# Attention inside a fused kernel: the six parts of `a` are added before one product with ones, and the maxima of phi move to another buffer

## The chip, the core and the metric

The kernel runs on one core of one Trainium2 chip. The core has a matrix engine (TensorE, written PE in the profile, with its weight loads as PEld), three engines for elementwise work (VectorE = DVE, ScalarE = ACT, GpSimd = POOL), and a sync engine (SP) whose queue issues all DMAs here. Each engine runs its own instruction list in order and waits on the others through semaphores. The metric is device time in microseconds.

## What is computed

Three stages follow each other. Only the first is touched; the other two are two feed-forward layers on its output (4608 tokens, width 512, hidden width 2048).

```
q, k, v: [8, 8, 576, 64]      phi: [8, 8, 576, 32]         (batch, heads, seq, ...)
a    = exp(phi - max over seq of phi);  a = a / (sum over seq of a + 1e-9)
k_m  = a^T k   [32, 64];  v_m = a^T v   [32, 64]           per batch and head
attn = softmax((q k_m^T) / 8);   x = attn v_m
y    = layer2(layer1(x))         layer1: (h - tanh h) w_out,  layer2: elu(h) w_out
```

The kernel leaves `a` undivided, and multiplies `k_m` and `v_m` by the reciprocal of the sum of `a` over the sequence afterwards.

## The kernel before, in words

**Units.** The attention is cut into 16 units; unit u is one batch and four of its heads. The 576 positions of the sequence lie as 96 partitions by 6 parts (`c`), so phi and `a` are tiles of 96 x 6 x 4 x 32. Unit 0 has tiles of its own (`at0`); units 1 to 15 share one set (`at1`).

**A unit's steps.** `unit` is a Python generator that emits instructions and yields; each `yield` ends a step. In order, for u >= 2 (`spaced`):

1. `top`, `cmax` (L120 to L122, DVE): maximum of phi over the six parts.
2. nothing (L126).
3. `mT` (PE transpose), `nmax`, `dmax` (DVE).
4. `bmax` (PE, L135); a yield of its own follows.
5. `bm` (ACT), then `a = phi - bm` (POOL for u >= 2, DVE for units 0 and 1).
6. load of the next phi.
7. `a = exp(a)` (ACT, L147).
8. `km`: 24 matmuls a^T [k v] into the PSUM tile `km` (L156), then six matmuls of `a[:, c]` with a tile of ones into its last columns (L159), which gives the sum of `a`. The trace shows every fp32 matmul as two records, so L156 is 48 records a unit, L159 12.
9. `rs`, `kk`, `vbd` (DVE, L165 to L171), the scaled k_m and v_m read from `km`.
10. and on: load of the next k and v; `pq`, `qT` twice; `kT_ps` (transposes of `kk` and `vbd`, L189 and L190), `kT`, `vm`; `sc` (scores) and its transpose; again `pq` twice and `sc`; `smax`; `exp`; a multiplication `s` (L215, POOL); `pT` (L218, DVE); `phl` (L222 on ACT, L223 on POOL); nothing; the stores of p.

Units 0 and 1 have no empty steps: their steps 8 and 9 are one.

**Rounds.** A driver calls one step of every live unit per round, in the order in which the units started. Unit u starts at a fixed round:

```
(0, 1, 7, 13, 19, 25, 32, 39, 45, 52, 58, 65, 78, 85, 92, 99)[u]
```

So step s of unit u runs in round start + s - 1, and three or four units are live at a time, a round's steps of the older unit ahead of those of the younger. The first 19 rounds are the prologue (with the conversion of the first weights, L48 to L60). After it, layer 1 runs as 64 blocks of two halves; each half emits an `h_unit` (PE, L343), its nonlinearity (ACT L354 to L357, POOL `v` L362, DVE L367 to L369, later ACT L375 and POOL `g` L376), two `x_unit` (PE L388, copied out by ACT L395), sometimes two `vw_half` (PE L328, ACT L331, DVE L333), and two rounds of units.

**Order.** The order of each engine's list is that of emission; nothing reorders it. A tile is taken from a pool by a tag; a tag of the pool `at_wk` has one buffer, so a new tile of the tag waits until every instruction that reads the old one is done, also one that is emitted after the new tile's first write. `top` has the tag `pT`, shared with the tile `pT`; `kk` and `vbd` have tags of their own. The PSUM tiles `mT`, `bmax`, `km`, `pq`, `kT_ps`, `sc`, `x_ps` and `vw_ps` share one pool of three buffers (after the prologue).

Of the kernel before, what the change touches and what calls it, by code (L numbers as in the profile page):

```python
# [8 lines left out]
F32 = mybir.dt.float32  # L9
# [4 lines left out]
ALU = mybir.AluOpType  # L14
# [4 lines left out]
B, H, S, D, M = 8, 8, 576, 64, 32  # L19
# [43 lines left out]
class Attention:  # L63
# [43 lines left out]
    def unit(self, u, nxt, eng, first_p=None):  # L107

        nc, wk, sm = self.nc, self.wk, self.sm
# [3 lines left out]
        kv, a, kT = self.kv, self.a, self.kT  # L113
        ps_tile = lambda shape, name: self.ps.tile(shape, F32, tag="m", name=name)

        ph = self.loaded.pop((u, "phi"))
        row = lambda name: wk.tile([128, 4, M], F32, tag="cmax", name=name)
        cmax = row("cmax")[:96]
        top = wk.tile([128, S], F32, tag="pT", name="top")[:96, :12 * M].rearrange("p (h c m) -> p h c m", h=4, c=3)
        nc.vector.tensor_tensor(top, ph[:, :, 0:3], ph[:, :, 3:6], op=ALU.max)  # L120
        nc.vector.tensor_tensor(cmax, top[:, :, 0], top[:, :, 1], op=ALU.max)
        nc.vector.tensor_tensor(cmax, cmax, top[:, :, 2], op=ALU.max)  # L122
        yield
        spaced = u >= 2
        if spaced:
# [10 lines left out]
        if spaced:  # L136
# [5 lines left out]
                          op=ALU.subtract)  # L142
# [9 lines left out]
        km = ps_tile([128, 2 * D + 2], "km")  # L152
        kmv = km[:, :2 * D].rearrange("p (t d) -> p t d", t=2)
        for c in range(6):
            for h in range(4):
                nc.tensor.matmul(kmv[32 * h:32 * h + 32], lhsT=a[:, c, h, :], rhs=kv[:, :, h, c, :],  # L156
                                 start=(c == 0), stop=(c == 5))
        for c in range(6):
            nc.tensor.matmul(km[:, 2 * D:], lhsT=a[:, c].rearrange("p h m -> p (h m)"), rhs=self.ones[:, :2],  # L159
                             start=(c == 0), stop=(c == 5))  # L160
        if spaced:
            yield
        rs = sm.tile([128, 1], F32, tag="rs", name="rs")
        twice = lambda t: kmv[:, t].rearrange("p (o d) -> p o d", o=1).to_broadcast([128, 2, D])
        nc.vector.tensor_scalar(rs, km[:, 2 * D:2 * D + 1], GUARD, None, op0=ALU.add)  # L165
        nc.vector.reciprocal(rs, rs)
        kk = wk.tile([128, 2, D], F32, tag="kk", name="kk")
        nc.vector.tensor_scalar(kk, twice(0), rs, None, op0=ALU.mult)
        vbd = wk.tile([128, 2, D], F32, tag="vbd", name="vbd")
        for j in range(2):  # L170
            nc.vector.tensor_scalar(vbd[:, j], kmv[:, 1], rs, self.pmask[:, j:j + 1], op0=ALU.mult, op1=ALU.mult)  # L171
        yield
# [2 lines left out]
        for pr in range(2):  # L175
# [25 lines left out]
            for hq in range(2):  # L201
                nc.tensor.matmul(sc[64 * hq:64 * hq + 64], lhsT=kT[:, 2 * pr + hq].rearrange("p c m -> p (c m)"),
                                 rhs=qT[:, hq].rearrange("p c q -> p (c q)"), start=True, stop=True)
# [13 lines left out]
        pT = wk.tile([128, S], F32, tag="pT", name="pT")  # L217
# [285 lines left out]
def moe_kernel(tc, q, k, v, phi, w1, w2, w3, w4, out):  # L503
    nc = tc.nc
    with ExitStack() as top, tc.manual_schedule():
# [96 lines left out]
        for u in range(2 * B):  # L602
            units.at((0, 1, 7, 13, 19, 25, 32, 39, 45, 52, 58, 65, 78, 85, 92, 99)[u], unit(u))
# [252 lines left out]
```

## Time and profile before

| | |
|---|---|
| time, median of 3 runs | 1750.95 us (1750.49 to 1754.13) |
| the profiled execution | 1751.26 us, span of its instructions 1749.5 us |
| PE / PEld busy | 1637.8 us (94%) / 1513.9 us (87%) |
| DVE busy | 1222.6 us (70%) |
| ACT busy | 954.2 us (55%) |
| POOL busy | 760.9 us (43%) |
| mean granted TensorE clock | 0.970 |

Attention takes part in the first 480 us or so of the span; the last unit's maxima are taken at 403.6 us and its `pT` is read at 478.4 us. A duration in a row is that of one instruction or of a merged run of like ones; "x12" is their number. A wait in brackets is the idle time of the engine ahead of the instruction, with the instruction that ended it.

### The profile page before, as it was taken

How to read it: one execution, taken by the hardware profiler on the slowest of the kernel's cores; microseconds unless marked ns; L12 is line 12 of the kernel's file. 1: busy time of each engine (PE TensorE's matmuls, PEld its weight loads, DVE VectorE, ACT ScalarE, POOL GpSimd, SP SyncE). 2: the span in 40 equal slices, each digit the busy share in tenths (PEclk: the TensorE clock that was granted, in tenths of full speed). 3: DMA queues.
4: the chain of work that ended last, by engine and by line, in shares of the span. 5: the costliest groups of instructions: out<-in, count | busy, mean ns of one | idle time of the engine just before them, and what ended most of it. 6: DMA issues, size and time to landing. Idle time of an engine off the chain costs nothing.

```text
span 1749.5 us, 30362 instructions
## 1 busy us (share of the span) xinstructions
PE 1637.8 (94%) x11632; PEld 1513.9 (87%) x11632; DVE 1222.6 (70%) x1821; ACT 954.2 (55%) x1713; POOL 760.9 (43%) x537
## 2 busy tenths in 40 slices
PE   5668989988998999999989999999999999999998
PEld 3557878887898999999989999999999999999997
DVE  5769666778899999998965555555555555555554
ACT  2456666677878888888863333333333333333332
POOL 2245545546666667676752222222222222222222
PEclk7669999999999999999999999999999999999999
DMA  8765555467566456666578312211212212111110
GB/s 213 198 177 148 179 158 181 147 199 232 187 211 200 167 182 208 215 223 208 203 230 316 130 60 61 61 54 56 61 61 61 61 61 61 58 52 58 58 31 25
DMA packets 140936, 238.42 MB, mean 136 GB/s; under 512 B 8184, under 2 KB 102392, under 8 KB 138744
## 3 DMA queue, kind: packets, MB, share of 16 engines
q1 hardware_dynamic: 140792, 236.49, 43.3%
q8 instruction: 92, 1.51, 0.4%
q14 instruction: 52, 0.43, 0.1%
HBM read 159.78 MB, written 75.50 MB: 134 GB/s over the span
## 4 chain that ended last, share of the span: by engine, by line
PE 75%; DVE 10%; ACT 5%; DMA 5%; issue 3%; POOL 2%; ACTq 0%; DVEq 0%; POOLq 0%; SPq 0%
PE h_ps L444 23%; PE o_ps L481 23%; PE x_ps L388 15%; PE h_ps L343 8%; PE vw_ps L328 3%; DVE s L368 2%; DMA w_dram<-wst 2%; DVE vw L333 1%; DMA raw<-in_moe_w_in_dram 1%; DMA phi<-in_phi_dram 1%; DVE h_ps L367 1%; DVE s L369 1%; PE km L156 1%; ACT t L354 1%; ACT big L357 1%
## 5 line engine op out<-in xcount | busy, mean ns | idle before, releaser
L388 PE MATMUL x_ps<-g,w 128*128 128x288 f32 x3072 | 442.8, 298 | 13.7 <-ACT x L395 6.7
L470 POOL TENSOR_TENSOR e<-hm,e 128x512 fp32r<-128x512 f32 x144 | 186.5, 1295 | 587.0 <-ACT e L469 442.6
L444 PEld LDWEIGHTS h_ps<-x,wi 128*128 128x128 f32 x3456 | 429.8, 190 | 11.7
L388 PEld LDWEIGHTS x_ps<-g,w 128*128 128x128 f32 x3072 | 421.5, 190 | 18.6 <-ACT x L395 8.0
L444 PE MATMUL h_ps<-x,wi 128*128 128x256 f32 x3456 | 433.2, 282 | 0.0
L481 PE MATMUL o_ps<-wo,e 128*128 128x512 f32 x1728 | 423.8, 394 | 0.7 <-POOL e L470 0.7
L481 PEld LDWEIGHTS o_ps<-wo,e 128*128 128x128 f32 x1728 | 314.9, 188 | 64.9 <-POOL e L470 1.1
L455 ACT ACTIVATE t_ps<-hm 128x512 f32<-128x512 f32 x144 | 86.7, 602 | 514.3 <-DVE hm L454 514.3
L362 POOL TENSOR_TENSOR v<-t,u 128x576 f32<-128x576 f32 x128 | 183.9, 1437 | 197.6 <-ACT u L355 163.9
L343 PE MATMUL h_ps<-p,vw 128*128 128x288 f32 x1536 | 235.8, 304 | 7.9 <-DVE s L369 6.3
L376 POOL TENSOR_TENSOR g<-s,g 128x576 fp32r<-128x576 f32 x128 | 199.0, 1555 | 96.1 <-ACT g L375 91.1
L461 DVE SCALAR_TENSOR_TENSOR hm<-hm,t_ps 128x512 f32<-128x512 f32 x144 | 99.1, 688 | 200.6 <-ACT hm L456 200.6
L343 PEld LDWEIGHTS h_ps<-p,vw 128*128 128x128 f32 x1536 | 217.0, 194 | 12.9 <-issue 7.9
L454 DVE TENSOR_SCALAR hm<-h_ps 128x512 f32<-128x512 f32 x144 | 99.6, 692 | 138.5 <-PE h_ps L444 138.5
L368 DVE SCALAR_TENSOR_TENSOR s<-s,v 128x576 f32<-128x576 f32 x128 | 139.9, 1093 | 3.7 <-POOL v L362 2.6
L354 ACT ACTIVATE t<-h_ps 128x576 f32<-128x576 f32 x128 | 83.2, 650 | 72.7 <-PE h_ps L343 28.4
L369 DVE COPY_PREDICATED s<-big,h_ps 128x576 f32<-128x576 uint32 x128 | 106.6, 833 | 12.0 <-ACT u L355 0.5
L333 DVE TENSOR_TENSOR vw<-vw_ps,vw 64x512 fp32r<-64x512 f32 x128 | 87.8, 686 | 36.5 <-ACT vw L331 34.5
L356 ACT ACTIVATE s<-u,bias 128x576 f32<-128x576 f32 x128 | 99.5, 778 | 24.0 <-POOL g L376 14.6
L328 PE MATMUL vw_ps<-w,vm 128*128 128x256 f32 x480 | 78.9, 304 | 28.2 <-ACT x L395 14.7
L463 DVE TENSOR_TENSOR hm<-hm,h_ps 128x512 f32<-128x512 f32 x144 | 99.0, 687 | 5.0
L462 DVE SCALAR_TENSOR_TENSOR hm<-hm,t_ps 128x512 f32<-128x512 f32 x144 | 98.9, 687 | 4.9
(85 smaller groups left out, 1827.5 us busy)
## 6 DMA issues: line engine op xcount, KB each, us to landing
x_dram<-x SPq DMA_DIRECT2D x128, 288.0 KB
xr<-x_dram SPq DMA_DIRECT2D x72, 512.0 KB
p<-p_dram SPq DMA_DIRECT2D x62, 576.0 KB
raw<-in_moe_w_in_dram SPq DMA_DIRECT2D x32, 512.0 KB
raw<-in_moe_w_out_dram SPq DMA_DIRECT2D x32, 512.0 KB
w_dram<-wst SPq DMA_DIRECT2D x32, 512.0 KB
kv<-in_k_dram SPq DMA_DIRECT2D x16, 576.0 KB
kv<-in_v_dram SPq DMA_DIRECT2D x16, 576.0 KB
```

The costliest lines, as they stand in the source:

```text
L328: nc.tensor.matmul(ps[:, kc], lhsT=vm[:, a, p, :], rhs=wi[:, b, p, :], start=(i == 0), stop=(i == 2))
L333: nc.vector.tensor_tensor(lo, src, r32(hi), op=ALU.subtract)
L343: nc.tensor.matmul(ps[:, j, :NB], lhsT=vw[a][:, kc, 128 * j:128 * j + 128], rhs=p[:, kc, b, :], start=(k == 0), stop=(k == 5))
L354: nc.scalar.activation(t, w[0], ACTF.Tanh)
L362: nc.gpsimd.tensor_tensor(v, t, u, op=ALU.mult)
L368: nc.vector.scalar_tensor_tensor(s, s, G_B, v, op0=ALU.add, op1=ALU.mult)
L369: nc.vector.copy_predicated(s, big.bitcast(U32), d)
L376: nc.gpsimd.tensor_tensor(g[:, 1], s, r32(g[:, 0]), op=ALU.subtract)
L388: nc.tensor.matmul(ps, lhsT=wo[pg][:, a, j, 128 * dm:128 * dm + 128], rhs=g[:, b, j, :], start=(k == 0), stop=(k == 11))
L444: nc.tensor.matmul(ps[:, j], lhsT=w3[:, a, kc, 128 * j:128 * j + 128], rhs=x[:, b, kc, :], start=(k == 0), stop=(k == 11))
L470: nc.gpsimd.tensor_tensor(e[:, 1], hm, r32(e[:, 0]), op=ALU.subtract)
L481: nc.tensor.matmul(self.acc[n][tg], lhsT=e[:, a, j, 128 * tg:128 * tg + 128], rhs=w4[:, b, j, :], start=(pg == 0 and j == 0 and i == 0), s ...
```

## The change

The maximum over the six parts of phi is taken in three DVE instructions of another shape, into a tile `top` of half the size that has the tag `kk`. After the 24 matmuls of `km`, three additions (on GpSimd for u >= 2, on DVE for units 0 and 1) sum the six parts of `a` into a tile `asum`, also of the tag `kk`; for u >= 2 a new `yield` follows; then one matmul of `asum` with ones takes the place of the six. `kk` and `vbd` become the two halves of one tile of the tag `kk`.

```
-        top = wk.tile([128, S], F32, tag="pT", name="top")[:96, :12 * M].rearrange("p (h c m) -> p h c m", h=4, c=3)
-        nc.vector.tensor_tensor(top, ph[:, :, 0:3], ph[:, :, 3:6], op=ALU.max)
+        pair = lambda name: wk.tile([128, 2, 4, M], F32, tag="kk", name=name)
+        top = pair("top")[:96].rearrange("p c h m -> p h c m")
+        nc.vector.tensor_tensor(top, ph[:, :, 0:2], ph[:, :, 2:4], op=ALU.max)
+        nc.vector.tensor_tensor(top, top, ph[:, :, 4:6], op=ALU.max)
         nc.vector.tensor_tensor(cmax, top[:, :, 0], top[:, :, 1], op=ALU.max)
-        nc.vector.tensor_tensor(cmax, cmax, top[:, :, 2], op=ALU.max)
         yield
...
-        for c in range(6):
-            nc.tensor.matmul(km[:, 2 * D:], lhsT=a[:, c].rearrange("p h m -> p (h m)"), rhs=self.ones[:, :2],
-                             start=(c == 0), stop=(c == 5))
+        asum = pair("asum")[:96]
+        add = nc.gpsimd if spaced else nc.vector
+        add.tensor_tensor(asum, a[:96, 0:2], a[:96, 2:4], op=ALU.add)
+        add.tensor_tensor(asum, asum, a[:96, 4:6], op=ALU.add)
+        add.tensor_tensor(asum[:, 0], asum[:, 0], asum[:, 1], op=ALU.add)
+        if spaced:
+            yield
+        nc.tensor.matmul(km[:, 2 * D:], lhsT=asum[:, 0].rearrange("p h m -> p (h m)"), rhs=self.ones[:96, :2],
+                         start=True, stop=True)
         if spaced:
             yield
...
-        kk = wk.tile([128, 2, D], F32, tag="kk", name="kk")
+        kkv = pair("kk").rearrange("p c h m -> p c (h m)").rearrange("p t (o d) -> p t o d", o=2)
+        kk, vbd = kkv[:, 0], kkv[:, 1]
         nc.vector.tensor_scalar(kk, twice(0), rs, None, op0=ALU.mult)
-        vbd = wk.tile([128, 2, D], F32, tag="vbd", name="vbd")
```

## Rows read from the trace of the kernel before

**Rows 1.** Busy time by stretch: the stretch in us from the span's start, its length, busy us (and instructions) of PE, PEld, DVE, ACT and POOL, the granted clock of TensorE as a share of full speed, the DMA share and GB/s.

```profile
0.00:61.50 61.50, 31.53 (x244) 22.64 (x244) 40.89 (x92) 18.84 (x42) 16.71 (x19) 0.65 0.80 202
...
400.00:480.00 80.00, 72.73 (x612) 67.21 (x611) 69.70 (x109) 63.32 (x122) 49.27 (x35) 1.00 0.65 212
...
61.50:480.00 418.50, 360.68 (x3006) 325.88 (x3006) 318.14 (x517) 283.35 (x555) 217.44 (x152) 0.95 0.60 181
480.00:1749.50 1269.50, 1245.56 (x8382) 1165.42 (x8382) 863.59 (x1214) 652.05 (x1117) 526.77 (x368) 0.99 0.36 118
```

**Rows 2.** The chain of work that ended last: its shares by line over the stretch 61.5 to 480 us, and three of its pieces of L159 (start, us, what). The last two are the first and the last of seven pieces of 1.43 us between 150 and 480 us.

```profile
by line: PE x_ps L388 14.5%; PE h_ps L343 10.2%; issue 7.6%; PE vw_ps L328 6.7%; DVE s L368 4.9%; PE km L156 3.1%; PE km L159 3.0%; DVE h_ps L367 2.9%; ACT big L357 2.9%; DVE vw L333 2.8%; ACT t L354 2.7%; DVE s L369 2.6%; DMA q<-in_q_dram 
...
122.94 2.65 PE km L159 x12
...
158.72 1.43 PE km L159 x12
...
435.60 1.43 PE km L159 x12
```

**Rows 3.** The matmuls with ones as one group of the costliest groups: records, busy us, mean ns of one, idle time before.

```profile
L159 PE MATMUL km<-ones,a 128*128 128x2 f32 x192 | 28.2, 275 | 0.0
```

**Rows 4.** Who waited for whom between 61.5 and 480 us, one line of DVE's and one of POOL's: us in total, times, the longest us.

```profile
DVE top L120 <- POOL phl L223: 20.1, 7, 7.0
...
POOL v L362 <- ACT u L355: 92.5, 29, 6.3
```

**Rows 5.** Instructions in order of time around the first step of unit 6 (its `top`): start, us, engine, line.

```profile
122.88 2.72 PE L159 MATMUL km<-ones,a 128*128 128x2 f32 x12
123.09 0.77 DVE L218 STREAM_TRANSPOSE pT<-s 128x576 f32<-128x576 f32 x1
...
126.88 0.68 PE L181 MATMUL pq<-ident,q 96*128 96x96 f32 x3
...
129.42 1.40 POOL L223 TENSOR_TENSOR phl<-pT,phl 128x576 fp32r<-128x576 f32 x1 [5.50 <-ACT phl L222]
...
130.86 0.56 DVE L120 TENSOR_TENSOR top<-phi 96x384 f32<-96x384 f32 x1 [7.00 <-POOL phl L223]
```

**Rows 6.** Instructions in order of time: `top` of units 10 and 12, and `top` of unit 14 with the `km` of unit 13 behind it.

```profile
246.47 0.55 DVE L120 TENSOR_TENSOR top<-phi 96x384 f32<-96x384 f32 x1 [4.68 <-POOL phl L223]
...
323.61 1.76 DVE L120 TENSOR_TENSOR top<-phi 96x384 f32<-96x384 f32 x1 [2.87 <-POOL phl L223]
...
373.87 0.54 DVE L120 TENSOR_TENSOR top<-phi 96x384 f32<-96x384 f32 x1
...
375.14 1.52 PE L156 MATMUL km<-kv,a 128*32 128x128 f32 x48
...
376.58 1.50 PE L159 MATMUL km<-ones,a 128*128 128x2 f32 x12
...
377.94 1.83 PE L388 MATMUL x_ps<-g,w 128*128 128x288 f32 x12
```

**Rows 7.** Durations in ns (shortest, median, longest) of single lines, for sizes: the subtraction of phi on POOL and on DVE, a POOL subtraction of the weights, and the maxima on DVE.

```profile
L141 POOL TENSOR_TENSOR a<-phi,bm x14: 1809/1856/2180, 37.5 to 425.0; 96x768 f32<-96x768 f32 x14
L141 DVE TENSOR_TENSOR a<-phi,bm x2: 954/954/955, 9.9 to 12.4; 96x768 f32<-96x768 f32 x2
...
L60 POOL TENSOR_TENSOR wst<-cv_a,wst x6: 1278/1289/1302, 399.5 to 475.7; 128x512 fp32r<-128x512 f32 x6
...
L120 DVE TENSOR_TENSOR top<-phi x16: 542/555/2029, 4.3 to 403.6; 96x384 f32<-96x384 f32 x16
...
L122 DVE TENSOR_TENSOR cmax<-cmax,top x16: 286/287/1530, 5.2 to 404.9; 96x128 f32<-96x128 f32 x16
```

**Rows 8.** The stretch 130 to 480 us: busy time of the engines as in rows 1, and the DVE instruction of L368 as a group (count, busy us, mean ns) and by its shortest, median and longest ns.

```profile
130.00:480.00 350.00, 314.12 (x2664) 287.74 (x2663) 269.63 (x431) 248.39 (x487) 188.25 (x131) 0.99 0.59 179
...
L368 DVE SCALAR_TENSOR_TENSOR s<-s,v 128x576 f32<-128x576 f32 x44 | 53.8, 1223 | 2.8 <-POOL v L362 1.7 <-ACT big L357 1.1
...
L368 DVE SCALAR_TENSOR_TENSOR s<-s,v x44: 739/759/3359, 133.2 to 477.6; 128x576 f32<-128x576 f32 x44
```

**Rows 9.** Waits of PE for a free PSUM buffer, 61.5 to 480 us: us in total, times, the longest us.

```profile
PE vw_ps L328 <- ACT x L395: 7.4, 10, 1.5
PE x_ps L388 <- ACT x L395: 6.7, 6, 1.4
...
PE vw_ps L328 <- DVE rs L165: 2.2, 2, 1.6
```

**Rows 10.** How long one unit (unit 9) holds its PSUM tile `km`: from the first matmul into it to the last read of it.

```profile
243.06 1.52 PE L156 MATMUL km<-kv,a 128*32 128x128 f32 x48
...
251.04 0.58 DVE L171 TENSOR_SCALAR vbd<-km,rs,pmask 128x64 f32<-128x64 f32 x2
```

**Rows 11.** The prologue: a piece of the chain (the DMA of phi for unit 2), three ACT instructions around the end of the prologue in order of time, and the wait of PE there.

```profile
16.53 11.69 DMA phi<-in_phi_dram
...
60.10 0.62 ACT L58 ACTIVATE w<-cv_a 128x512 fp32r<-128x512 f32 x1
...
61.18 0.28 ACT L196 ACTIVATE vm<-kT_ps 128x128 fp32r<-128x128 f32 x1
...
63.39 0.59 ACT L331 ACTIVATE vw<-vw_ps 64x512 fp32r<-64x512 f32 x1 [1.93 <-PE vw_ps L328]
...
PE vw_ps L328 <- ACT vm L196: 5.3, 1, 5.3
```

## The prediction

> **What bounds the kernel now.** I read the busy time by stretch first. Up to 61.5 us PE is busy for half of the time; from 61.5 to 480 us, where 14 of the 16 units run between the blocks of layer 1, it is busy 360.7 of 418.5 us (86%); from 480 us on 1245.6 of 1269.5 us (98%), with work that the change doesn't touch [rows 1]. So whatever the attention stretch gains or loses goes to the end unshrunk, and inside the stretch there are 58 us in which PE waits. The chain of waits comes next: between 61.5 and 480 us it changes from PE to DVE and ACT and back within every block, and the matmuls with ones hold 3.0% of it, 12.6 us [rows 2]. No single engine sets the end there: in the last 80 us PE is busy 91% and DVE 87% [rows 1]. What DVE waits for I read from its waits: 20.1 us in front of `top`, all on POOL's `phl` [rows 4].
>
> **Matmuls with ones.** 192 records become 32 (12 to 2 a unit), 28.2 us of PE busy time [rows 3] becomes about 28.2 x 2/12 = 4.7. What counts is what lies on the chain: one unit at 2.65 us and seven at 1.43 us [rows 2]; 10/12 of 2.65 + 7 x 1.43 = 12.7 is 10.5 us. The others end behind DVE or DMA work: unit 0's and unit 1's lie under the DMA of phi that the next `top` waits for, 16.53 to 28.22 us [rows 11]. The paths beside PE are close behind (DVE at 87%), so I take 9 of the 10.5; bounds 3 and 10.5.
>
> **Maxima.** Before, 384 and twice 128 elements a partition: 0.555 + 2 x 0.287 = 1.13 us [rows 7]. After, twice 256 and once 128; by the line through 0.287 (128) and 0.555 (384) 256 cost 0.42, so again 1.13. Nothing on DVE.
>
> **The wait of `top`.** This is where the change is least obvious. Seven `top`s wait for `phl` because they write the buffer of `pT`. That `top` waits even for readers emitted after it is to be seen at unit 6: `pT` of unit 3 is written in the same round just ahead, `phl` is emitted a round later, and DVE stands still from 123.86 to 130.86 us [rows 5]. In the changed kernel `top` is out of that buffer, so the 20.1 us go [rows 4]. But it is now in the buffer of `asum`, and the same thing happens there. Unit u emits `asum` in round start + 7; the matmul that reads it is behind the new yield, in round start + 8. Where unit u + 1 starts 7 rounds after unit u (u = 5, 6, 8, 10, 12, 13, 14), its `top` is emitted in round start + 7 too, after `asum`, so `top` takes the buffer next and DVE must wait for a matmul that PE comes to a round later. Where the gap is 6 or 13, `top` is ahead of `asum` or far behind it, and waits for nothing new. Seven waits go, seven come.
>
> Their size: at unit 14 DVE reaches `top` at 373.87 us, ahead of unit 13's `km` on PE, which ends at 376.58 [rows 6]. PE then has an `x_unit` (1.8 us) and a `pq` (0.68 us at the lower clock of [rows 5], some 0.4 here) before the matmul of `asum`: about 378.8, so 4.9 us of DVE standing still where there was no wait. Worked out in the same way from the time at which DVE reaches `top` and from PE's list up to the next round, the seven are 1.7 (unit 6, instead of 7.0), 2, 3.5, 3.6, 2.5, 4.9 and 3.1: 21 us. The waits of units 10 and 12, 4.68 and 2.87 us [rows 6], go without a successor. Sum 21 against 20.1. Behind the waiting `top` in DVE's list stand the `d`, `s` and predicated copy of the half (L367 to L369), which free PE's `h_ps` only two halves later, and the `vw` copies. I charge +1; bounds -6 (two of the old waits of 2.87 us ended on the chain, the new ones hidden) and +15 (all 21, less those 5.7).
>
> **The additions.** On GpSimd 768 elements take 1.86 us and 512 take 1.28 [rows 7], 2.26 ns an element: 256, 256 and 128 give 0.70 + 0.70 + 0.41 = 1.8 us a unit, 25 us in 14 units. POOL is busy 217 of 418 us [rows 1], and stood idle 92.5 us in front of `v` alone, waiting for ACT [rows 4], so its own list hides them. The price is elsewhere: L368 on DVE takes 0.739 us alone and 1.223 in the mean, up to 3.359 [rows 8], and the long ones fall on POOL's subtractions. 44 x 0.484 = 21.3 us of stretch against 188 us of POOL work is 0.11 us per us; 25 us more of POOL stretch DVE by 2.9. DVE is on the chain for part of the time: +1.0, bounds 0 and 2.9. That stretch is what the Trainium skill (GPSIMD Engine Reference, section 8, Key points) states: GpSimd shares its SBUF interfaces with VectorE and contends with DVE instructions that have two SBUF inputs; the trace agrees in the 3.359 us of an instruction that takes 0.739 alone. For units 0 and 1 the additions are on DVE, 0.42 + 0.42 + 0.29 = 1.13 us beside the 24 `km` matmuls (1.52 us at unit 9 [rows 10], more at the prologue's granted clock of 0.65 [rows 1]): nothing.
>
> **One yield more.** Everything from `rs` on comes a round later, with its DMAs (next k and v, next q, stores of p) and their place in SP's queue. The nearest user is three rounds off (k and v asked for in round start + 10, read in round start + 13 at the earliest), so none is late. A round is 4.1 us: units 6 and 15 end `km` 276.9 us apart [rows 2] and 67 rounds. What it costs is PSUM: `km` is held for 8.6 us now [rows 10] and 8.6 + 4.1 - 1.2 then, and while it is held the others share two buffers. PE's waits for buffers are 16.3 us [rows 9]. 14 units x 2.9 us = 41 us more of holding; if the waits came evenly over 418 us that is 1.6, if only while `km` is held (14 x 8.6 = 120 us) 5.6. I take 2.5; bounds 0 and 5.6.
>
> **End of the prologue.** Unit 2's `kT` and `vm` slip from its last round into the first block. PE's wait of 5.3 us there was for `vm` [rows 11], and goes; but the copy of `vw` can start only after ACT's `w` at 60.7 instead of at 63.39, and of those 2.7 us about half is left once the fourth `vw` waits for a buffer, so the first `h_unit` comes some 1.4 us earlier; the moved ACT work (0.28 us of `vm` and two copies like it, 0.8 us) delays what follows. -0.5; bounds -1.4 and +0.8.
>
> **Sum.** -9 + 1 + 1 + 2.5 - 0.5 = -5.0 us against the profiled execution (1751.26 us with 1.8 us around its span): 1746.3. The median of the runs shown is 0.3 us lower, so 1746. This measurement can tell about 0.2%, 3.5 us, from no change.
>
> **The rivals.**
>
> *Stall.* The new waits of `top` fall on the path in full: -9 + 15 + 1 + 2.5 - 0.5 = +9, 1760. For it: DVE 87% busy in the last 80 us, so that 3 to 5 us are not caught up before the next. Against it: 7.0 us at unit 6 before did not stop PE by as much. It decides the sign for the measurement once the waits cost more than about 9.5 us net. Chance 0.2.
>
> *Contention.* Every us by which POOL stretches DVE reaches the end: -9 + 1 + 2.9 + 2.5 - 0.5 = -3.1, 1748: no change to be told. For it L368's 4.9% of the chain [rows 2]; against it DVE's own waits, which take up some. The rule of the Trainium skill named above (GPSIMD Engine Reference, section 8) is this rival's. Chance 0.12.
>
> *Pace.* ACT and DVE set the pace of a half, and PE waits where it worked: only 3 of the 10.5 us arrive: -3 + 1 + 1 + 2.5 - 0.5 = +1, 1752. For it the 58 us of PE idle; against it that the chain gives PE most of the pieces. Chance 0.13.
>
> *Free DVE.* The old waits were worth more than the chain shows and the new ones hide: -9 - 6 + 0 + 0 - 0.5 = -15.5, 1735. Chance 0.13.
>
> **How the numbers follow.** The forecast has 0.42, its own range 1741 to 1750; about seven tenths of it lie beyond -3.5 us. Faster: 0.13 + 0.3 = 0.43, and 0.02 from contention: 0.45. Slower: 0.2 and a little of pace and forecast: 0.24. Same: 0.31. From 1736 to 1757 all but the outer parts of stall and free DVE are held.
>
> **What would show it.** Two records of L159's successor per unit; POOL additions of 0.70 and 0.41 us; no `top` waiting for `phl`; seven `top`s (units 6, 7, 9, 11, 13, 14, 15) waiting on PE's `km`, 2 to 5 us each; PE's wait for `vm` near 61 us gone; more waits of PE on ACT's `x`. The prediction is wrong if those seven waits are absent (then free DVE), if they exceed 30 us or stop `h_unit`s (stall), or if PE's idle time between 61.5 and 480 us grows by what its busy time falls (pace).

## The result, and the profile after

The changed kernel is slower: 1771.79 us in the median (1764.15 to 1777.14) against 1752.54 for the kernel before on the same chip, a ratio of 1.0114 with a 95% interval of 1.009 to 1.0138, some 20 us. The forecast was 1746, with 1736 to 1757 as its range. A thousandth of the time is 1.75 us; ratios below are all to the kernel before, run beside the kernel in question.

The profiled execution after took 1768.98 us. Busy time by stretch, columns as in [rows 1]:

```profile
0.00:61.50 61.50, 28.38 (x230) 20.44 (x230) 42.72 (x95) 16.56 (x35) 17.33 (x21) 0.75 0.72 178
61.50:120.00 58.50, 31.11 (x207) 23.78 (x207) 43.00 (x72) 27.04 (x56) 25.39 (x21) 0.62 0.74 192
...
61.50:480.00 418.50, 337.74 (x2731) 300.24 (x2732) 311.57 (x491) 269.29 (x534) 233.26 (x181) 0.90 0.58 175
480.00:1767.00 1287.00, 1260.37 (x8514) 1178.89 (x8512) 881.63 (x1242) 668.24 (x1146) 540.00 (x378) 1.00 0.37 120
```

Between 61.5 and 480 us PE is busy 337.7 us instead of 360.7 [rows 1], at a granted clock of 0.90 instead of 0.95. Of these 23.0 us, 16.4 are the matmuls with ones themselves (21.1 us in this stretch before, 4.7 after); besides, 132 more records of PE run behind 480 us, where PE is 98% busy as before. The groups that replace L159 [rows 3] and the waits that answer to [rows 4] are these (groups: count, busy us, mean ns, idle before; waits: total, times, longest):

```profile
L166 PE MATMUL km<-ones,asum 96*128 96x2 f32 x32 | 6.5, 272 | 8.7 <-POOL asum L163 8.5
...
L161 POOL TENSOR_TENSOR asum<-a 96x256 f32<-96x256 f32 x14 | 12.4, 884 | 5.6 <-DVE cmax L123 5.6
L162 POOL TENSOR_TENSOR asum<-asum,a 96x256 f32<-96x256 f32 x14 | 11.0, 789 | 1.1
L163 POOL TENSOR_TENSOR asum<-asum 96x128 f32<-96x128 f32 x14 | 6.3, 453 | 1.1
```

```profile
DVE top L121 <- PE km L166: 25.6, 7, 4.5
...
PE km L166 <- POOL asum L163: 8.5, 5, 4.1
...
PE h_ps L350 <- DMA p<-phl: 3.7, 1, 3.7
```

The matmuls shrank from 28.2 to 6.5 us, and the seven waits of `top` are there, 25.6 us. Two waits of PE are new: for the sum on POOL, and at the first `h_unit` for a DMA.

Compared by the predicated copy of each half (L369 before, L376 after), DVE's first one comes 6 us later than before, at 82 instead of 76 us; then 2.3 us later at the seventh (161 us), 11.9 at the ninth (175 us), 18.5 at 479 us, and 18 to 22 from 490 us on. So there are at least two losses: one at the prologue's end and one in the blocks.

**The first loss.** The end of the prologue in order of time, first before and then after: SP's issues of k, v and p, DVE's `phl` of unit 1, and the first `h_unit`.

```profile
46.65 0.33 SPq L97 DMA_DIRECT2D kv<-in_k_dram  x1
...
59.78 0.76 DVE L223 TENSOR_TENSOR phl<-pT,phl 128x576 fp32r<-128x576 f32 x1 [1.29 <-ACT phl L222]
60.57 2.44 SPq L230 DMA_DIRECT2D p<-phl  x4
...
66.69 1.79 PE L343 MATMUL h_ps<-p,vw 128*128 128x288 f32 x12
```

```profile
60.47 0.40 SPq L97 DMA_DIRECT2D kv<-in_k_dram  x1
60.91 1.19 SPq L98 DMA_DIRECT2D kv<-in_v_dram  x1
...
61.75 0.76 DVE L230 TENSOR_TENSOR phl<-pT,phl 128x576 fp32r<-128x576 f32 x1 [1.29 <-ACT phl L229]
62.54 2.44 SPq L237 DMA_DIRECT2D p<-phl  x4
...
66.02 1.65 PE L335 MATMUL vw_ps<-w,vm 128*128 128x256 f32 x6 [5.28 <-DVE vw L340]
...
71.41 3.22 PE L350 MATMUL h_ps<-p,vw 128*128 128x288 f32 x12 [3.74 <-DMA p<-phl]
```

Before, SP asked for the next k and v at 46.65 us; `phl` started at 59.78 and the first `h_unit` at 66.69, 6.9 us later, and took 1.79 us. After, k and v (2 x 576 KB) are asked for at 60.5 us, right ahead of the p that the first block needs, and the `h_unit` comes 9.7 us behind `phl` and takes 3.22 us.

**The second loss.** Around `top` of unit 7, in order of time:

```profile
165.46 1.75 PE L395 MATMUL x_ps<-g,w 128*128 128x288 f32 x12
168.61 0.39 ACT L402 ACTIVATE x<-x_ps 128x288 f32<-128x288 f32 x1
169.06 0.47 PE L188 MATMUL pq<-ident,q 96*128 96x96 f32 x3 [1.85 <-ACT x L402]
169.36 0.31 PE L166 MATMUL km<-ones,asum 96*128 96x2 f32 x2
...
169.65 1.42 POOL L230 TENSOR_TENSOR phl<-pT,phl 128x576 fp32r<-128x576 f32 x1
169.70 1.64 DVE L121 TENSOR_TENSOR top<-phi 96x256 f32<-96x256 f32 x1 [4.53 <-PE km L166]
170.02 1.65 PE L335 MATMUL vw_ps<-w,vm 128*128 128x256 f32 x6 [0.35 <-ACT qT L190]
...
171.02 1.58 POOL L383 TENSOR_TENSOR g<-s,g 128x576 fp32r<-128x576 f32 x1
...
171.38 1.50 DVE L122 TENSOR_TENSOR top<-top,phi 96x256 f32<-96x256 f32 x1
...
173.24 1.42 DVE L340 TENSOR_TENSOR vw<-vw_ps,vw 64x512 fp32r<-64x512 f32 x2
173.99 3.25 PE L395 MATMUL x_ps<-g,w 128*128 128x288 f32 x12 [2.32 <-DVE vw L340]
```

It goes in a circle. DVE stands before `top` until PE comes to the ones-matmul; PE is held ahead of it by a PSUM buffer that ACT frees at 169.0; DVE then reaches the `vw` copies only at 173.24, and PE waits 2.32 us for the buffer that these free, and the next `x_unit` takes 3.25 instead of 1.75 us. Besides, `top` then runs beside POOL's `phl` and `g`, and its two instructions take 1.64 and 1.50 us. In `e2_own` (below), where `top` waits for nothing at this step, they take 0.38 and 0.42 us:

```profile
166.22 0.38 DVE L121 TENSOR_TENSOR top<-phi 96x256 f32<-96x256 f32 x1
...
166.63 0.42 DVE L122 TENSOR_TENSOR top<-top,phi 96x256 f32<-96x256 f32 x1
```

The circle is not the whole of what DVE falls back here. Between the seventh and the ninth copy `e2_own` falls back too, from 3.5 to 7.9 us behind the kernel before, the changed kernel from 2.3 to 11.9.

### The profile page after: what moved, and what is told of

It is laid out like the page before. It is cut to its first block, busy times and chain, and to the rows that moved or that the text cites. A ratio compares the mean times of both kernels' runs of the same rounds, so it can differ in the third digit from the quotient of the medians.

```text
span 1767.2 us, 30108 instructions
## 1 busy us (share of the span) xinstructions
PE 1626.5 (92%) x11472; PEld 1499.6 (85%) x11472; DVE 1235.9 (70%) x1827; ACT 954.1 (54%) x1713; POOL 790.6 (45%) x579
## 4 chain that ended last, share of the span: by engine, by line
PE 65%; DMA 6%; DVE 3%; ACT 2%; issue 2%; POOL 1%; ACTq 0%; SPq 0%; DVEq 0%; POOLq 0%
PE h_ps L451 23%; PE o_ps L488 22%; PE x_ps L395 11%; PE h_ps L350 6%; DMA p<-p_dram 3%; PE vw_ps L335 2%; DMA raw<-in_moe_w_in_dram 1%; DMA w_dram<-wst 1%; DMA xr<-x_dram 1%; DVE s L375 1%; ACT vw L338 0%; DVE s L376 0%; ACT t L361 0%; DVE h_ps L374 0%; DVE vw L340 0%
## 5 line engine op out<-in xcount | busy, mean ns | idle before, releaser
L369 POOL TENSOR_TENSOR v<-t,u 128x576 f32<-128x576 f32 x128 | 184.0, 1438 | 201.5 <-ACT u L362 161.5
L350 PE MATMUL h_ps<-p,vw 128*128 128x288 f32 x1536 | 239.8, 307 | 12.2 <-issue 5.6
L350 PEld LDWEIGHTS h_ps<-p,vw 128*128 128x128 f32 x1536 | 221.0, 197 | 16.5 <-issue 12.7
L375 DVE SCALAR_TENSOR_TENSOR s<-s,v 128x576 f32<-128x576 f32 x128 | 134.6, 1052 | 5.7 <-POOL v L369 4.7
L376 DVE COPY_PREDICATED s<-big,h_ps 128x576 f32<-128x576 uint32 x128 | 106.5, 832 | 11.6
L340 DVE TENSOR_TENSOR vw<-vw_ps,vw 64x512 fp32r<-64x512 f32 x128 | 87.8, 686 | 31.7 <-ACT vw L338 29.7
```

Of the source, the lines that this page charges most:

```text
L350: nc.tensor.matmul(ps[:, j, :NB], lhsT=vw[a][:, kc, 128 * j:128 * j + 128], rhs=p[:, kc, b, :], start=(k == 0), stop=(k == 5))
L369: nc.gpsimd.tensor_tensor(v, t, u, op=ALU.mult)
L375: nc.vector.scalar_tensor_tensor(s, s, G_B, v, op0=ALU.add, op1=ALU.mult)
L376: nc.vector.copy_predicated(s, big.bitcast(U32), d)
```

## The experiments

Three theories are weighed in the expectations: *stall* (the seven waits of `top` on the ones-matmul), *yield* (the round more) and *GpSimd* (PE's wait for the sum, and POOL's added work).

**One part at a time: the maxima, the yield, the matmuls.** `e4_maxima` is the kernel before with the maxima alone moved; `kk` and `vbd` are the two halves of one tile, as in the changed kernel.

```
 (before)
+        pair = lambda name: wk.tile([128, 2, 4, M], F32, tag="kk", name=name)
+        top = pair("top")[:96].rearrange("p c h m -> p h c m")
```

> The kernel before with the maxima alone moved: top in the buffer of kk and vbd (made one), six ones-matmuls on TensorE, no sum on GpSimd, no extra yield. What the 20.1 us of DVE's old waits for phl are worth. If DVE's waits in front of top set the pace of a block: 1738 to 1745. If they were hidden (DVE catches up before PE needs it): 1750 to 1754. All three theories allow either; stall needs the old waits to have been hidden less than the new ones.

Measured: 1.0006 (0.9994 to 1.0018). DVE's 20.1 us of waits for `phl` are gone from its trace (3.4 us of waits for the DMA of phi stand in their place), and nothing came of it: before, they cost nothing that can be measured.

`e1_six`:

```
 (changed kernel)
-        asum = ...; add.tensor_tensor(...) x3
         if spaced:
             yield
-        nc.tensor.matmul(km[:, 2 * D:], lhsT=asum[:, 0]..., rhs=self.ones[:96, :2], ...)
+        for c in range(6): nc.tensor.matmul(km[:, 2 * D:], lhsT=a[:, c]..., rhs=self.ones[:, :2], ...)
```

> The changed kernel with the six ones-matmuls a unit put back on TensorE and the three additions left out; the extra yield and the maxima in the buffer of kk stay. No top then stands behind a matmul that PE comes to a round later. Theory 'stall' (the seven waits of top on the ones-matmul, 25.6 us, cost the 19 us): about 1745 to 1755, since the waits go and the 10 us of matmuls return, while the old waits on phl (20.1 us) are gone too. Theory 'yield' (the round more, with the prologue's later first h_unit and the longer hold of PSUM, costs it): 1772 to 1780, since nothing of the cost goes and the matmuls return. Theory 'GpSimd' (PE waits for POOL's sum, 8.5 us, and POOL's added 30 us stretch DVE): about 1752 to 1758.

Measured: 1.0011 (0.9993 to 1.0028). The loss needs the sum on GpSimd or the waits of `top` on its matmul; the yield and the moved maxima, with all six matmuls, cost no more than 5 us together.

`e6_one` (`for c in range(1)` in the kernel before):

> The kernel before with one of the six ones-matmuls of a unit kept (the first) and five left out, nothing put in their place: the sum of phi's features is over one sixth of the rows only. The worth of the matmuls by themselves. If they lie on the path as the chain of waits gave them: 1739 to 1742 (9 to 10.5 us). If DVE and ACT set the pace where they run ('pace'): 1746 to 1751.

Measured: 0.9973 (0.9958 to 0.9988), 4.7 us faster. That is what the matmuls are worth in the kernel before, and about the most that the change could win.

**The waits of `top`.** `e2_own`:

```
 (changed kernel)
-        cmax = row("cmax")[:96]
-        top = pair("top")[:96].rearrange("p c h m -> p h c m")
+        top = wk.tile([128, 2, 4, M], F32, tag="cmax", name="top")[:96].rearrange("p c h m -> p h c m")
+        cmax = top[:, :, 0]
```

> The changed kernel with top in the buffer of cmax (made twice as wide) instead of that of kk and asum; the sum on GpSimd and the extra yield stay. top waits for nothing of PE. Stall: 1742 to 1752, the 25.6 us of DVE's waits in front of top gone. Yield: 1762 to 1770, with the first h_unit still at about 71 us instead of 66.7 and the granted clock of 61.5 to 120 us still at 0.62. GpSimd: 1760 to 1770, with PE's wait for POOL at the ones-matmul still 8 us or more.

Measured: 1.0053 (1.0041 to 1.0065), 1757.97 us, between the ranges of the three theories. The waits account for 0.0061 of the 0.0114, 10.7 us; what is left points to the other two theories.

`e12_pT` and `e15_six_pT` put `top` of the changed kernel and of `e1_six` back into the buffer of `pT`:

```
-        top = pair("top")[:96].rearrange("p c h m -> p h c m")
+        top = wk.tile([128, S], F32, tag="pT", name="top")[:96, :8 * M].rearrange("p (c h m) -> p h c m", c=2, h=4)
```

> The changed kernel with top put back into the buffer of pT; asum keeps the buffer of kk. The seven waits on the ones-matmul (25.6 us) go and the old waits on POOL's phl (about 20 us) come back. Theory 'whom it waits for' (a wait of DVE on PE's own later work stops PE, which stands behind DVE's copies; a wait on POOL is caught up): as e2_own, 1756 to 1759. Theory 'a wait is a wait': 1768 to 1772, as the changed kernel.

Measured: 1.0164 (1.0141 to 1.0188), 1777.53 us, slower than the changed kernel. My theory that it matters for whom DVE waits fell. The waits for `phl`, which is a round later here, are not 20.1 but 31.5 us (DVE's waits of e12_pT, then of e15_six_pT):

```profile
DVE top L121 <- POOL phl L230: 31.5, 7, 6.0
```

```profile
DVE top L121 <- POOL phl L226: 31.6, 7, 6.3
```

> e1_six (six ones-matmuls, extra yield, no additions; 1.0011) with top in the buffer of pT, so that it waits for phl again, which is a round later than in the kernel before. If the waits of top cost because they are longer than the block's slack (31.5 us in e12_pT against 20.1 before): about 30 us of waits again and 1765 to 1775. If they cost only where TensorE has fewer matmuls to run meanwhile: 1751 to 1756.

Measured: 1.0129 (1.0102 to 1.0156) against 1.0011 for `e1_six`, which differs by this buffer alone: 20.6 us for 31.6 us of waits, with six matmuls too. So seven waits cost nothing at 20.1 us, 10.7 us at 25.6 and about 20 at 31.5. They are not the same seven: those of units 6, 7 and 9 to 13 before, of 6, 7, 9, 11, 13, 14 and 15 in the changed kernel, of 7, 8, 9, 11, 12, 13 and 15 in these two. The reading that fits is slack, which was not used up before; no run measures it by itself. Where it lies the waits show in part: before, the longest one (7.0 us) fell at 124 to 131 us, where PE is busy 73% of the time (18.34 of the 25 us from 110 to 135 us), and two were under 0.5 us; in `e12_pT` six of the seven are 2.9 us or more and begin behind 165 us, and from 200 to 480 us PE is 85% busy there.

**The sum on GpSimd.** `e3_noyield`, the changed kernel without its new yield:

> The changed kernel without the extra yield: the ones-matmul stands in PE's list right behind the 24 matmuls of km, so PE waits there for POOL's sum, and top of the next unit waits for a matmul that is reached in the same round. Stall: the seven waits of top shrink from 25.6 us to about 10, time 1757 to 1765. Yield: 1745 to 1755, the prologue's first h_unit back at about 66.7 us. GpSimd: PE's wait for POOL grows from 8.5 us to 14 units x about 2.5 us = 35 us, time 1775 to 1790.

Measured: 1.0234 (1.0216 to 1.0251), 41 us slower:

```profile
PE km L164 <- POOL asum L163: 40.6, 13, 4.4
DVE top L121 <- PE km L164: 23.2, 6, 5.5
```

The loss is as long as PE's wait, but six waits of `top` on the same matmul are in it too (about 10 us of them were expected, 23.2 came), and so is what the matmuls give; what each of them cost is not shown. The yield is there for PE's wait, and what it leaves is 8.5 us. In `e7_dead` POOL adds, and nobody reads the sum:

```
 (e1_six, with top in the buffer of cmax)
+            asum = pair("asum")[:96]; nc.gpsimd.tensor_tensor(...) x3
```

> e1_six (six ones-matmuls, extra yield; 1751.6) with top in the buffer of cmax and with the three additions of units 2 to 15 on POOL as in the changed kernel, their result read by nothing: nobody on PE waits for POOL. Contention theory: POOL's 14 x 2.1 = 30 us more stretch DVE by some 3 us and delay v on POOL, time 1755 to 1760. If POOL's work is hidden and only PE's wait for it costs: 1750 to 1753.

Measured: 1.002 (1.0004 to 1.0037), 0.0009 above `e1_six`, 1.6 us with an interval of about -3 to 6: POOL's load has no price that is clear of nothing.

`e11_dve` (`add = nc.vector` for all units):

> e2_own with the three additions on DVE for all units (1.13 us each unit, 16 us of DVE in the blocks) in place of POOL. PE waits for asum: DVE comes to them sooner than POOL, PE's wait shrinks below 9 us, but DVE is busy 77% of 61.5 to 480 us: 1752 to 1757. If POOL's contention was the price: 1748 to 1752. If DVE's time is what sets the pace: 1762 to 1770.

Measured: 1.0055 (1.0034 to 1.0076), as `e2_own`; no gain from taking POOL out. `e9_early` and `e10_early_y`:

```
 (e5_six01; its additions go up)
         nc.scalar.activation(av, av, ACTF.Exp)
+        if spaced:
+            asum = ...; nc.gpsimd.tensor_tensor(...) x3
         yield
...
-            yield
         one matmul
```

`e9_early` takes out the extra yield ahead of the ones-matmul (last lines), `e10_early_y` leaves it in.

> Built on e5_six01 (top in cmax's buffer, six ones-matmuls for units 0 and 1): for units 2 to 15 the additions on POOL stand right behind Exp, a round ahead of km, and the extra yield is gone, so the order of the blocks is that of the kernel before. Theory 'PE waits for asum' (the 8.8 us in six places of e5_six01 are most of its 9 us of loss): 1746 to 1751, with that wait under 3 us. Theory 'POOL's list' (POOL, in order, now stands still for Exp and holds v and g back): 1753 to 1760, with POOL's waits for ACT a at the additions above 20 us.

> e9_early with the extra yield put back: the sum is emitted two rounds ahead of the ones-matmul. PE waits for asum: 1747 to 1752, with no wait of PE for asum left and km a round later as in e1_six (1.0011 of before). POOL's list: as e9_early. If the yield itself is the price: 1753 to 1756 against e9_early's 1746 to 1751.

Measured: `e9_early` 1.0002 (0.9987 to 1.0016), `e10_early_y` 1.0047 (1.003 to 1.0064). In `e10_early_y` PE never waits for the sum, and it is slow; in `e9_early` it does, and it is not:

```profile
PE km L166 <- POOL asum L154: 10.7, 8, 2.1
```

So PE's 8 to 10 us of waiting for POOL were not the price: they can have cost little more than the matmuls gave. What goes with the loss is the yield.

**The yield in unit 2.** `e5_six01` and `e8_six012` keep six matmuls for the first two units, and for the first three with no extra yield in unit 2:

```
 (e2_own; e5_six01: "if u >= 2", e8_six012: "if u >= 3")
+        if u >= 3:
             asum = ...; add x3; yield; one matmul
+        else: six matmuls
```

> e2_own (top in the buffer of cmax) with the six ones-matmuls kept for units 0 and 1, so that DVE makes no additions in the prologue; units 2 to 15 as in e2_own. Theory 'DVE bounds the prologue' (there it stands still for under 3 us between 30 and 62 us in e1_six and in e2_own, and everything on it comes 2.4 us later in e2_own at 59 us): 1753 to 1756, the first h_unit some 2.5 to 3 us earlier than in e2_own's 71.25 us. Theory 'GpSimd' (the 8 us that e2_own still loses against the kernel before come from units 2 to 15: PE's wait of 9.3 us for POOL's sum and the stretch of DVE): 1757 to 1758.

> e2_own with the change for units 3 to 15 only: units 0, 1 and 2 keep six ones-matmuls and no extra yield, so that the prologue's order is that of the kernel before. If what e2_own loses (8 us) is lost at the prologue's end: 1746 to 1751, and below the kernel before if the matmuls are worth anything. If it is lost in the blocks: 1756 to 1758.

Measured: 1.0054 (1.0031 to 1.0077) and 1.0019 (1.0002 to 1.0036). DVE's additions in the prologue cost nothing that can be measured; leaving unit 2 as it was gives 6 us back. `e14_unit2` gives unit 2 of `e8_six012` the yield and not the sum:

> e8_six012 (1.0019; sum on POOL from unit 3 on) with the extra yield in unit 2 too, whose six ones-matmuls stay. If the yield in unit 2 is the price: 1756 to 1759, as e5_six01 (1.0054). If unit 2's sum on POOL is (PE waits 3.5 us for it at 108 us in e5_six01): 1751 to 1754, as e8_six012.

Measured: 1.0039 (1.0021 to 1.0058): a little over half of the way to `e5_six01`; the intervals leave both, and the yield is the likelier. `e13_kvload` leaves the yield and moves one line of `e2_own`:

```
-        yield
         self.load(nxt, "kv")
+        yield
```

> e2_own (1.0053) with one line moved: a unit's load of the next k and v is emitted ahead of the last yield before it, in the round in which the kernel before emits it; all else of e2_own, the yield too, stays. Theory 'DMA order' (in the yield kernels the k and v of unit 3 are asked for at 57 to 61 us instead of 47, just ahead of unit 1's p, and the first h_unit comes 9.6 to 10.4 us behind phl instead of 7): the load is back at about 47 us, the first h_unit about 7 us behind phl with no wait for p, time 1751 to 1755. Rival 'order of the engines' (kT, vm and what follows slip into the first block and delay it whatever the DMA does): 1757 to 1759.

Measured: 1.0005 (0.9991 to 1.002). One line takes 0.0048, 8.4 us, and its trace shows where:

```profile
47.29 0.33 SPq L97 DMA_DIRECT2D kv<-in_k_dram  x1
...
61.11 0.76 DVE L230 TENSOR_TENSOR phl<-pT,phl 128x576 fp32r<-128x576 f32 x1 [1.29 <-ACT phl L229]
61.90 2.43 SPq L237 DMA_DIRECT2D p<-phl  x4
...
66.83 3.08 PE L350 MATMUL h_ps<-p,vw 128*128 128x288 f32 x12
```

The `h_unit` of `e2_own`:

```profile
71.25 3.22 PE L350 MATMUL h_ps<-p,vw 128*128 128x288 f32 x12 [4.32 <-DMA p<-phl]
```

`phl` is as late as in `e2_own` (61.01 us there), kT and vm of unit 2 are still in the first block, yet the first `h_unit` starts 5.7 us behind `phl` without a wait; in `e2_own` it starts 10.2 us behind it, at 71.25 us, after 4.3 us of waiting for p. That is the order of the DMAs. The line moves the loads of every unit, but `e2_own` stands 4.6 us behind `e13_kvload` at the first predicated copy already, and 6.4 us at 479 us.

All other traces agree on the wait. Every kernel with the late load, `e1_six` and `e7_dead` too, stands 3.5 to 4.5 us for p there and starts its first `h_unit` 9.4 to 10.4 us behind `phl`; every kernel without it starts 5.7 to 7.2 us behind `phl`, with no such wait. (Only the distance can be read: `phl` itself starts anywhere between 58.2 and 62.8 us.) The price of the wait is not one number. `e1_six` and `e7_dead` have it and stand at 1.0011 and 1.002; in `e7_dead` the first copy comes 7.6 us later than before, the one at 479 us only 3.4.

**Do the two prices add, and is there a faster kernel?** `e18_after_kv` is the changed kernel with that one line, `e17_early_kv` is `e10_early_y` with it.

> The changed kernel with the load of the next k and v emitted a yield earlier, the one line of e13_kvload; top stays in the buffer of asum and waits for the ones-matmul as before. If the two prices add: 1.0114 less 0.0048 is 1.0066 of before, 1760 to 1764, the seven waits of top still 25 us. If the waits of top take up what the earlier first block gives: 1768 to 1772.

Measured: 1.0089 (1.0063 to 1.0114), between the two expectations: 0.0025 given back where 0.0048 was expected, and with some 0.0035 of noise on the difference that is not clear of nothing. The seven waits are the same, 25.6 us. The two profiled executions show where the gain goes: the first predicated copy comes 3.0 us earlier than in the changed kernel, the one behind unit 6's wait of `top` (138.5 us in the changed kernel) only 1.3, and it stays at 1.3 to 1.6.

> e10_early_y (top in the buffer of cmax, six ones-matmuls for units 0 and 1, the sum on POOL right behind Exp, two rounds ahead of its matmul; 1.0047) with the load of the next k and v in the round of the kernel before. No wait of PE for asum, none for the late p. If the matmuls' 4.7 us come through once both prices are gone: 1744 to 1748. If POOL's work and the later rs and kT take them: 1749 to 1753.

Measured: 1.0012 (0.9987 to 1.0036). Faster than `e10_early_y` by 0.0035, no faster than the kernel before. `e16_ones_in_kv` leaves GpSimd out of it:

```
 (before)
-        self.kv = fix.tile([128, 2, 4, 6, D], ...)
+        self.kv = fix.tile([128, 2, 4, 6, D + 1], ...)      # column D holds ones
-            nc.sync.dma_start(out=t[:96, 0], in_=view("k", 0, 4))   (and v)
+            for h in range(4): for i, n in enumerate("kv"):
+                nc.sync.dma_start(out=t[:96, i, h, :, :D], in_=view(n, h, 1)[:, 0])
-        six ones-matmuls
```

> The kernel before without the six ones-matmuls: k and v get a 65th column of ones in SBUF, so that the 24 matmuls of km (130 columns instead of 128) give the sums themselves; no GpSimd, no yield. The loads of k and v are eight DMAs of 256-byte rows instead of two of 1536-byte rows. If the loads stay hidden: 1744 to 1749, as e6_one (0.9973). If the smaller rows make them late, in the prologue above all: 1755 to 1770.

Measured: 0.999 (0.9972 to 1.0009), 1750.05 us. It wins nothing that can be told; the eight issues fill SP's queue from 48.68 to 53.97 us, still ahead of p. No kernel here beats the one before by more than its interval but `e6_one`, which leaves work out.

## Why the prediction was wrong, point by point

- **Matmuls with ones, -9: mis-sized.** Records fell as worked out and busy time to 6.5 us (4.7 were worked out), but the matmuls are worth 4.7 us (`e6_one`, 2.1 to 7.4). The chain of waits gave them 12.6 us [rows 2]; its pieces show what came last, not what follows when it is shortened. The range's lower bound of 3 was sound, the choice of 9 next to its top was not. DVE at 87% [rows 1] was the warning; that DVE is what held the rest back is argued and not tested. The sign named for *pace* could not tell it: over a window of fixed length PE's idle time grows by what its busy time falls, whatever the cause.
- **Maxima, 0: right by themselves** (`e4_maxima`: 27.3 us of DVE busy time in three groups, 25.6 before, and no change of the time). In the changed kernel they take 34.1 us, in `e2_own`, without the waits, 31.6; at unit 7 they run beside POOL's work.
- **The wait of `top`, +1: the step that failed in the blocks.** The seven waits came, in the places named and near the size worked out (25.6 us for 21). What failed was the netting: "seven waits go, seven come", each at the same price. The old ones were worth nothing (`e4_maxima`), the new ones 10.7 us (`e2_own`). The rival *stall*, with +15 for this term, had the mechanism; its 1760 falls short by what the first block lost.
- **The additions, +1.0: right in size as far as can be told, wrong in one sentence.** They took 29.7 us of POOL, 25 were worked out; `e7_dead` gives 0.0009, 1.6 us, not clear of nothing. The rule of the Trainium skill that was weighed there (GPSIMD Engine Reference, section 8, Key points) is not contradicted (`top` beside POOL's `phl` and `g` agrees with it: 1.64 and 1.50 us, against 0.38 and 0.42), but no run here tells its effect on the time from none. "Its own list hides them" was wrong: POOL does the additions in its list's order, and from 102.6 us it stood 3.85 us for ACT in front of `s` with the additions behind it. PE waited 4.1 us for that, and 8.5 us in five places. `e9_early`, with 10.7 us of such waits, is no slower than the kernel before; `e3_noyield`, with 40.6 us of them and 23.2 us of waits of `top`, is 41 us slower.
- **One yield more, +2.5, and end of the prologue, -0.5: the step that failed first.** "The nearest user is three rounds off (...), so none is late" asked when the moved k and v are needed, and not what is queued behind them. One round is 4.1 us in a block but 13 us at the end of the prologue (47.3 against 60.5 us), and there the 1.15 MB of k and v went in ahead of the p of the first block. PE's wait for `vm` went, as said; one of 5.28 us for a buffer of `vw` took its place, and 3.74 us for p came behind it. One line of order is 8.4 us in `e2_own` (`e13_kvload`) and 0.0035, 6 us, in `e10_early_y`; in the changed kernel itself it is 0.0025, not clear of nothing (`e18_after_kv`). What the term had worked out for the engines holds once the load is back: the first `h_unit` starts 5.7 us behind `phl` instead of 6.9, 1.2 us sooner where 1.4 were worked out, but it runs at the lower clock (last section). PSUM hold, the reason given for +2.5, can't be told apart: `e13_kvload` keeps the yield and stands at 1.0005, with the 4.7 us of the matmuls spent on this and on other things.
- **The sum.** Along the kernels, 0.0005 from before to `e13_kvload`, 0.0048 to `e2_own` (the load), 0.0061 to the changed kernel (the waits): 0.0114, the whole. By the other way round (`e13_kvload`, `e18_after_kv`, the changed kernel) the waits are 0.0084 and the load 0.0025: by these ratios the two prices overlap, and no single division of the 20 us can be read off. In the first step the 4.7 us of the matmuls have gone against POOL's load, PE's waits for the sum and the later `rs`; of these some 4 us have no run of their own, and how they divide is not settled. Nor is why the late load costs less with six matmuls in all units (`e1_six`, `e7_dead`: 1.0011 and 1.002) than with one.

## What to carry to other kernels

When a yield moves a step, look at the issue queue at every place where the moved DMA now lands, the first block above all, and ask what stands behind it, not only when its data is needed. Waits of one engine cannot be netted by their microseconds: the price of a wait depends on the slack left at its place, and 20 us may be free where 25 cost 11. Read a stretch of the chain of waits as a bound of what its removal gives: 12.6 us on the chain were worth 4.7 here. A next engine that is nearly as busy is the warning.

## What the runs showed of the hardware

What a wait of PE costs is not only its length: behind two of them the changed kernel ran at the lower clock. Stretches of it, columns as in [rows 1]: the six `vw` matmuls ahead of the first `h_unit`, behind 5.28 us of standing still; that `h_unit`, behind 3.74 us more; the `x_unit` ahead of the wait at 169 us; the `vw` matmuls behind that wait; and the next `x_unit`.

```profile
66.02:67.67 1.65, 1.65 (x6) 1.36 (x6) 1.34 (x2) 0.00 (x0) 0.00 (x0) 0.50 1.12 285
...
71.40:74.60 3.20, 3.19 (x13) 3.18 (x14) 0.00 (x0) 0.00 (x0) 0.00 (x0) 0.50 1.06 305
165.50:167.20 1.70, 1.70 (x13) 1.47 (x12) 0.00 (x0) 1.19 (x2) 0.34 (x2) 1.00 0.25 103
170.00:171.70 1.70, 1.65 (x6) 1.35 (x6) 1.67 (x2) 0.54 (x1) 1.70 (x2) 0.50 0.64 183
174.00:177.20 3.20, 3.20 (x14) 2.92 (x14) 2.90 (x4) 0.00 (x0) 0.00 (x0) 0.50 0.99 259
```

The granted clock is 0.50, 0.50, 1.00, 0.50 and 0.50 (0.50 is 1.2 GHz, 1.00 is 2.4 GHz), and the same twelve matmuls take 3.2 us at the one level and 1.7 to 1.8 at the other. Both times the clock was low already ahead of the second wait (3.74 and 2.32 us). At 170 us it had fallen behind 1.85 us of standing still. Not every wait did this: the kernel before stood 1.53 us at 154 us and ran on with six `vw` matmuls in 0.98 us, where the changed kernel's took 1.65 at 170 us.

```profile
154.13 0.98 PE L328 MATMUL vw_ps<-w,vm 128*128 128x256 f32 x6 [1.53 <-ACT x L395]
```

None of the forecast's terms had the clock in it. It has its own part in the first loss, beside the order of the DMAs: in `e13_kvload`, with no wait for p, the first `h_unit` takes 3.08 us too. The stretches of that `h_unit`, and of the first one of the kernel before:

```profile
66.83:69.91 3.08, 3.08 (x14) 3.06 (x14) 0.69 (x1) 0.59 (x1) 0.00 (x0) 0.50 1.00 302
```

```profile
66.70:68.50 1.80, 1.80 (x16) 1.64 (x16) 1.24 (x2) 0.59 (x1) 0.00 (x0) 1.00 0.86 267
```

Ahead of it PE had stood 5.20 us and worked 1.65 us in `e13_kvload`; in the kernel before it had stood 5.32 us and worked 5.34 us.
